# Attention and mixture-of-experts attention on one core: a planner that counts instruction fetches, and its new order

## The chip, the cores and the metric

One core of a Trainium2 chip runs the whole program. The metric is the device time of one execution in microseconds (us). The times shown are the median of three runs; the profile is of one further execution.

## The reference, cut to what matters

Causal softmax attention over 4 batches of 12 heads (448 positions, 64 wide); its output, heads side by side (768 wide), is the input x of a layer of four experts, each a causal attention head of its own, of which a gate takes two per position.

```python
scores = scale * q @ k.T ; causal mask ; a = softmax(scores) ; x = a @ v      # 48 heads
logits = x @ w_gate                     # the two best of 4 experts, softmax over them: w
for e in range(4):
    q, k, v = x @ wq[e], x @ wk[e], x @ wv[e]
    ye = softmax(causal(scale * q @ k.T)) @ v @ wo[e]
    out += chosen_e * w_e * ye
```

All is float32. The projections split weights and x into a high and a low part and take three products (fp32r); scores and softmax times v are plain fp32, whose matmuls the trace records twice.

## The kernel before, in words

The kernel is written as a list of 1540 steps (`Op`), each with the engines that can take it, a duration for each, the steps it comes after, and the buffers that it uses. Nothing is looped over at run time: `Plan.run` goes through the steps in the hand-kept list `ORDER`, gives each to the engine that would end it first by the planner's own clock (or to the one that `CHOSEN` pins), finds buffers, and emits the instructions there and then. So `ORDER` sets, for every engine, the order of its queue, and which buffer a step reuses. The durations (`T_...` and the numbers in `add(...)`) are never seen by the chip; they steer only which engine and which buffer a step gets.

Heads go in pairs: one "member" is two heads (64 partitions each), numbered 0 to 23 for the first layer (6 a batch); members 24 to 31 are the second layer's (batch, experts two by two). A "couple" of two members shares a softmax for the last 64 rows. By name, with the engine that runs them:

- `s1`, `s2` (TensorE, line 532): the scores of one block of 128 rows, and of two blocks; 20 and 40 instructions (weight loads and matmuls). `sq` (line 562): the last 64 rows of a couple, 16 instructions. These and `pv` use TensorE in quarters of 64 x 64.
- `max` (VectorE, line 444), `exp` (ScalarE, line 450), `eps` and `r` (sum and reciprocal), `rg` (GpSimd, times the gate), `norm` (GpSimd or ScalarE, lines 362 and 360): the softmax.
- The turn of the probabilities: for most couples `tr` on VectorE (line 478) and four quarter moves by DMA; for the couples 0 and 4 of the first layer and for the last one (members 30 and 31) transposes `tr` on TensorE (line 501, up to four blocks each) and a copy `mv` out of PSUM by ScalarE or VectorE.
- `pv` (TensorE, line 653): a couple's probabilities times v, 68 calls of matmul, which are 272 instructions. `xh`, `xl`, `xr`: its result copied out in a high and a low part.
- `pj` (line 714): a third of a projection to q or k, 12 instructions. `pjv` (line 761): half of a projection to v and gate, 18 or 12. `pjo` (line 857): the output projection, 12 (in the last batch in two halves of 6). `hb`, `vb`, `ob`: their copies; `gate`: the choice of experts (lines 814 to 839).
- `ld`, `wl`, `mv`, `st`: DMAs, all issued from SyncE's queue (one at the start from ScalarE's).

A step's number after the colon (pv:14) is its first member; pj, pjv and pjo count by batch. The planner's `run` adds `SWITCH` where TensorE changes between whole-array and quarter steps, doubles TensorE's durations before `COLD`, and adds fixed lags between engines. It knows nothing of how instructions reach the engines. Six warm-up matmuls (line 919, 24 instructions) go ahead of the first step of TensorE.

Of the kernel before, what the change touches and what calls it, by code (L numbers as in the profile page):

```python
# [35 lines left out]
class Op:  # L36
    def __init__(self, name, kind, on, emit, after, bufs):
        self.name, self.kind, self.on, self.emit = name, kind, dict(on), emit
        self.after = [a for a in after if a is not None]
        self.bufs = list(bufs)  # L40
        self.size, self.depth = 0.0, 0.0
        if "DMA" in on:
            self.on["DMA"], self.size, self.depth = on["DMA"]
        self.end, self.engine, self.tiling = 0.0, None, 0
        for b in self.bufs:
            b.users += 1
# [11 lines left out]
class Plan:  # L58
# [7 lines left out]
    FROM_PE, FROM_REST, FROM_DMA, SWITCH = 0.22, 0.2, 0.1, 0.11  # L66
    LANDING = 2.0
    SHARED = ("lo", "w", "norm")

    def __init__(self, homes):  # L70
        self.ops = []
        self.homes = homes

    def add(self, name, kind, on, emit, after=(), bufs=(), tiling=0):
        op = Op(name, kind, on, emit, after, bufs)
        op.tiling = tiling
        self.ops.append(op)
        return op

    def seen(self, ops, e):  # L80
        lag = {"PE": self.FROM_PE, "DMA": self.FROM_DMA}
        return max((a.end + (lag.get(a.engine, self.FROM_REST) if a.engine != e or e == "DMA" else 0.0) for a in ops), default=0.0)

# [15 lines left out]
    def run(self, order, chosen, make, tiles):  # L99
        free = dict(self.BEGIN)  # L100
        slots = defaultdict(list)
        copied, last = self.BEGIN["DMA"], None
        for n in order:
            op = self.ops[n]
# [17 lines left out]
            if e == "PE":  # L122
                last = op
            if port:
                free["port"] = end
# [14 lines left out]
def tile_attention_then_moe_attention(  # L140
# [85 lines left out]
    class Make:  # L226
# [12 lines left out]
    QUARTERS = 1  # L239
    LAST = (B - 1,)  # L240
    GROUPS = ((1,), (0, 2))
    ORDER = (
# [726 lines left out]
```

## Time and profile before

| what | us |
|---|---|
| median of 3 runs | 265.44 (264.3 to 267.62) |
| the profiled execution's own time | 263.77 |
| its span, first to last instruction | 262.0 |
| TensorE busy | 249.5 |
| VectorE busy | 203.0 |
| ScalarE busy | 175.4 |
| GpSimd busy | 137.0 |

In the rows PE is TensorE's matmuls, PEld its weight loads, DVE VectorE, ACT ScalarE, POOL GpSimd, SP SyncE. The span was profiled on the one core; its granted TensorE clock is 0.998 of full speed over the span. "issue" is idle time in which an engine waited for nothing that the profile shows. Ends of matmuls are modelled, so short waits between them can lie inside TensorE's busy time.

### The profile page before, as it was taken

The numbers are of one execution on the slowest core, as the hardware profiler recorded it, in microseconds if no ns is written. First come the engines' busy times: TensorE is split into PE (matmuls) and PEld (weight loads), VectorE is DVE, ScalarE is ACT, GpSimd is POOL, SyncE is SP. The second block draws the span as 40 slices with busy tenths as digits, with TensorE's granted clock in tenths as the row PEclk, the third lists the DMA queues.
The fourth block names the chain that finished last, engine by engine and source line by source line (L and its number), as shares of the span: only waits on it lengthen the run. The fifth ranks groups of instructions, "written<-read, shape, count | busy, mean of one in ns | idle before, by whom it ended". The sixth has DMA issues, their size and how long they took to land.

```text
span 262.0 us, 10480 instructions
## 1 busy us (share of the span) xinstructions
PE 249.5 (95%) x4065; PEld 215.8 (82%) x4065; DVE 203.0 (77%) x725; ACT 175.4 (67%) x600; POOL 137.0 (52%) x303
## 2 busy tenths in 40 slices
PE   7999997699999999999998999999999999999992
PEld 5678786579988879998987888989789898989892
DVE  5999999388879998899896998779796654574221
ACT  3999999849465879488584798546365533973321
POOL 6599988479961177975901854860801700043000
PEclk9999999999999999999999999999999999999999
DMA  6997889579878888788858548978868157013317
GB/s 200 397 399 228 206 229 345 191 211 239 220 165 218 232 269 195 220 201 254 256 163 221 139 110 228 271 219 229 200 168 195 34 116 172 0 53 121 115 70 280
DMA packets 34177, 52.27 MB, mean 199 GB/s; under 512 B 3664, under 2 KB 30160, under 8 KB 34128
## 3 DMA queue, kind: packets, MB, share of 16 engines
q1 hardware_dynamic: 33984, 51.47, 68.7%
q8 instruction: 32, 0.52, 0.8%
q10 hardware_dynamic: 144, 0.13, 0.2%
q14 instruction: 17, 0.14, 0.2%
HBM read 19.67 MB, written 5.51 MB: 96 GB/s over the span
## 4 chain that ended last, share of the span: by engine, by line
PE 92%; ACT 3%; issue 3%; DVE 0%; DVEq 0%
PE ps L714 23%; PE ps L653 20%; PE ps L532 15%; PE ps L761 13%; PE ps L857 11%; PE ps L562 5%; PE ps L501 4%; ACT five L450 2%; PE ps L919 1%; ACT tee L450 0%; ACT five L354 0%; DVE raw L356 0%; ACT raw L354 0%; ACT stat L460 0%; DVE five L444 0%
## 5 line engine op out<-in xcount | busy, mean ns | idle before, releaser
L450 ACT ACTIVATE five<-five,stat 128x256 f32<-128x256 f32 (+2 forms) x192 | 95.3, 499 | 33.0 <-DVE stat L444 30.2
L362 POOL TENSOR_SCALAR five<-five,stat 128x128 f32<-128x128 f32 (+2 forms) x171 | 79.7, 486 | 33.0 <-DVE stat L465 16.6
L444 DVE CUSTOM_DVE_ANT_0 five<-ps,mask 128x256 f32<-128x256 f32 (+2 forms) x156 | 59.2, 413 | 15.3 <-PE ps L532 14.9
L714 PE MATMUL ps<-two,wqkh 128*128 128x448 f32 x192 | 55.7, 371 | 0.0
L532 PE MATMUL ps<-raw 64*64 64x128 f32 (+5 forms) x768 | 51.0, 362 | 2.2 <-issue 1.5
L478 DVE STREAM_TRANSPOSE five<-five 128x768 f32<-128x768 f32 x52 | 48.7, 958 | 2.7 <-POOL five L362 1.4
L532 PEld LDWEIGHTS ps<-raw 64*64 64x64 f32 x768 | 32.6, 134 | 12.6 <-issue 6.8
L653 PE MATMUL ps<-five,v 64*64 64x64 f32 (+2 forms) x960 | 38.2, 277 | 1.7 <-issue 1.6
L714 PEld LDWEIGHTS ps<-two,wqkh 128*128 128x128 f32 x192 | 34.4, 188 | 4.2 <-DVE two L356 0.7
L450 ACT ACTIVATION_READ_ACCUMULATOR five<-five,stat 128x1 f32 x192 | 36.4, 190 | 0.0
L653 PEld LDWEIGHTS ps<-five,v 64*64 64x64 f32 x960 | 31.8, 134 | 4.9 <-issue 2.4
L714 PE MATMUL ps<-two,wqkl 128*128 128x448 f32 x96 | 35.1, 366 | 0.0
L761 PE MATMUL ps<-wvh,two 128*128 128x260 f32 x168 | 33.1, 286 | 0.0
L761 PEld LDWEIGHTS ps<-wvh,two 128*128 128x128 f32 x168 | 27.4, 188 | 2.1 <-issue 1.6
L354 ACT ACTIVATE raw<-ps 128x448 f32<-128x448 f32 (+1 forms) x31 | 15.2, 505 | 19.5 <-PE ps L714 11.2
L857 PE MATMUL ps<-two,woh 128*128 128x448 f32 x96 | 27.8, 371 | 0.0
L761 PE MATMUL ps<-wvl,two 128*128 128x260 f32 x96 | 26.4, 283 | 0.0
L653 PE MATMUL ps<-tee,v 64*64 64x64 f32 x672 | 25.6, 218 | 0.4 <-issue 0.4
L653 PEld LDWEIGHTS ps<-tee,v 64*64 64x64 f32 x672 | 23.3, 134 | 1.0 <-issue 0.5
L532 PE MATMUL ps<-warm 64*64 64x64 bf16 x192 | 21.7, 190 | 2.2 <-issue 2.2
L366 DVE TENSOR_TENSOR two<-ps,two 128x448 fp32r<-128x448 f32 x32 | 19.1, 616 | 5.3 <-ACT two L354 5.1
L450 ACT ACTIVATE tee<-tee,stat 128x448 f32<-128x448 f32 x32 | 21.0, 659 | 1.0 <-DVE stat L444 1.0
(93 smaller groups left out, 443.0 us busy)
## 6 DMA issues: line engine op xcount, KB each, us to landing
five<-five SPq DMA_DIRECT2D x104, 192.0 KB, 3.7
raw<-in_qk_dram SPq DMA_DIRECT2D x23, 448.0 KB, 6.0
tee<-tee SPq DMA_DIRECT2D x52, 112.0 KB, 3.5
v<-in_v_dram SPq DMA_DIRECT2D x24, 224.0 KB, 4.3
out_dram<-raw SPq DMA_DIRECT2D x9, 448.0 KB, 2.8
raw<-in_wqk_dram SPq DMA_DIRECT2D x4, 384.0 KB, 6.3
out_dram<-raw SPq DMA_DIRECT2D x6, 224.0 KB, 2.8
raw<-in_wvg_dram SPq DMA_DIRECT2D x2, 390.0 KB, 6.0
```

The costliest lines, as they stand in the source:

```text
L354: nc.scalar.activation(out, in_, AF.Copy)
L362: (nc.gpsimd if e == "POOL" else nc.vector).tensor_scalar(t, t, r, 1.0, op0=ALU.mult, op1=ALU.mult)
L366: eng.tensor_tensor(out=out, in0=a, in1=b, op=ALU.subtract)
L444: lambda e: nc.vector.tensor_tensor_reduce(out=w(), in0=scored(), in1=masked(), scale=-0.125, scalar=3.0e38, op0=ALU.add, op1=ALU.min, acc ...
L450: lambda e: nc.scalar.activation(w(), w(), AF.Exp, bias=stat.at[:, 0, u:u + 1], scale=-1.0, accum_out=stat.at[:, 1, u:u + 1],), [mx], [sto ...
L478: nc.vector.transpose(grouped(mid.at)[:, ks], squares(store.at)[:, ks])
L532: nc.tensor.matmul(out(c, h, lo, hi), lhs, rhs, start=(c, h) not in first, stop=True, skip_group_check=True)
L562: nc.tensor.matmul(tails[h ^ m.n].at[sides[m.n], :S], t.at[sides[h], REM:REM + R], t.at[sides[h], KEY], start=True, stop=True,)
L653: nc.tensor.matmul(o, ms[n].vals(h, k), t, start=(step == 0), stop=(step == len(runs[0]) - 1), skip_group_check=True)
L714: nc.tensor.matmul(ps.at[:, :S], w[:, 2 * sel + p, k], halves(xbuf[b, k].at, t), start=(k == 0 and n == 0), stop=(k == NP - 1 and n == 2),)
L761: nc.tensor.matmul(ps.at[:, :VC], xbuf[b, k].at[:, at + c * P:at + c * P + P], w[:, k], start=(k == 0 and n == 0), stop=(k == NP - 1 and n ...
L857: nc.tensor.matmul(ps.at[:, :S], w[:, p, m * P:m * P + P], halves(ubuf[b, p].at, t), start=(p == 0 and n == 0), stop=(p == 1 and n == 2),)
```

## The change

The planner gets a model of how TensorE's instructions arrive: blocks of 256, asked for 64 ahead of a block's end, 6.0 us each and one behind another; a step that reads over a boundary before its block is there is given a later end. Each TensorE step carries its number of instructions (`words`). Some durations are corrected. `ORDER` and `CHOSEN` are replaced by lists searched with this planner. The steps themselves, their instructions and their dependences are the same.

```diff
-    FROM_PE, FROM_REST, FROM_DMA, SWITCH = 0.22, 0.2, 0.1, 0.11
+    FROM_PE, FROM_REST, FROM_DMA, SWITCH = 0.22, 0.2, 0.1, 0.14
+    BLOCK, AHEAD, FETCH, FIRST = 256, 64, 6.0, 30
...
+        self.read, self.asked, self.needed, self.coming = self.FIRST, self.BLOCK - self.AHEAD, 2 * self.BLOCK, []
...
+    def fetch(self, start, d, words):
+        late, end = 0.0, self.read + words
+        while min(self.asked, self.needed) <= end:
+            at = min(self.asked, self.needed)
+            now = start + d * (at - self.read) / words + late
+            if at == self.asked:
+                self.coming.append(max([now] + self.coming) + self.FETCH)
+                self.asked += self.BLOCK
+            else:
+                late += max(0.0, self.coming.pop(0) - now)
+                self.needed += self.BLOCK
+        self.read = end
+        return d + late
...
             if e == "PE":
                 last = op
+                end = start + self.fetch(start, end - start, op.words)
...
-    T_EXP = (0.39, 0.50, 0.60, 0.71)
-    T_NORM = (0.35, 0.46, 0.57, 0.67)
-    T_NORMA = (0.29, 0.40, 0.51, 0.62)
+    T_EXP = (0.39, 0.495, 0.60, 0.655)
+    T_NORM = (0.35, 0.46, 0.56, 0.62)
+    T_NORMA = (0.30, 0.40, 0.51, 0.57)
-    T_TURNT = 1.02
+    T_TURNT = 1.035
...
-            add(("vb", NC * b + c), "vx", {"POOL": 0.5, "ACT": 0.45}, lambda e: cross(e, 0), made[:NF], [vb, vx]),
+            add(("vb", NC * b + c), "vx", {"POOL": 0.6, "ACT": 0.45}, lambda e: cross(e, 0), made[:NF], [vb, vx]),
...
-        return made, add(("gate", b), "gate", {"DVE": 1.3}, rest, [x], [gt, big])
+        return made, add(("gate", b), "gate", {"DVE": 1.5}, rest, [x], [gt, big])
```

Words given: s1 20, s2 40, sq 16, pv 4 x 68, pj 12, pjv 6 for each of its terms, pjo 12 or 6, transposes 2 for each block. Steps pinned to an engine: ScalarE 81 before and 92 after, VectorE 26 and 26, GpSimd 51 and 50.

The order of TensorE's 231 steps, read out of the two lists (x2: twice in a row). Before:

```
s1:0x3 s1:1 sq:0 s2:1 sq:2 s2:2 s1:3 s1:2 tr:0 s1:4 s1:5 sq:4 s2:4 tr:0 s2:3 tr:0 tr:1 tr:0x2 s2:5 tr:1x2 s2:7 s1:7
pv:0 tr:4 sq:8 s1:8 sq:6 s2:8 tr:4 pj:1 pj:0 s2:6 s1:6 tr:4x3 tr:5x3 s2:9 s1:9 pv:2 sq:10 pv:4 s2:10 s1:10 pj:0 pj:1
pj:0 s2:11 sq:12 s1:11 pj:1 pjv:0x2 pjv:2 pj:2 pjv:2 pjv:1x2 pj:2 s1:24 s2:24 pv:6 s2:12 s1:12 pjv:3 pj:3x2 pj:2 pj:3
s1:13 s2:13 pv:8 sq:24 s1:15 pjv:3 pj:5 s1:25 s2:25 s2:15 pj:5 pj:4x2 sq:14 pv:10 s2:14 pjv:5 pjv:6 pjv:5 pj:5 pjv:4x2
pjv:6 pj:4 s1:14 s1:16 sq:16 pv:12 s2:17 s2:16 s1:17 pjv:7x2 pj:6x2 pj:7 pj:6 sq:18 s1:19 pv:24 s1:18 s2:19 s2:18
pj:7x2 pjo:3 pjo:5 pjo:4 pjo:2 sq:26 s1:26 pv:14 s1:27 s2:27 s2:26 pjo:0 pj:9 pjv:8 pj:9 s1:20 s2:20 sq:22 pv:16 sq:20
pj:8x2 s1:21 s2:21 pj:9 pjv:8 pjo:1 pjv:10 pj:8 pjv:10 s2:23 s1:23 pv:18 s1:22 s2:22 pj:10 pj:11x3 pj:10 pjv:11 pjv:9
pj:10 pjv:11 pv:26 s1:28 s2:28 sq:28 pjv:9 pj:14 pjo:6 pjo:8 s2:29 pv:20 s1:29 pj:13 pj:15 pjv:13 pj:15 pj:12 pjv:14
pj:13 pv:22 pj:12 pj:14 pj:13 pj:15 pj:12 pj:14 pjv:14 s1:30 s2:30 s1:31 sq:30 s2:31 pjv:13 pjv:15x2 pjv:12 pjo:11
pjv:12 pjo:7 pv:28 pjo:9 pjo:10 pjo:16 pjo:17 tr:30x3 pjo:15 tr:31x2 tr:30 tr:31 tr:30 pjo:14 pv:30 pjo:12 pjo:13
pjo:21x2 pjo:23 pjo:22 pjo:20x2 pjo:23 pjo:19 pjo:22 pjo:18x2 pjo:19
```

After:

```
s1:0x3 s1:1 sq:0 s1:2 s2:1 s1:3 s2:2 s1:4 sq:2 tr:0x3 s2:4 sq:4 s2:3 s2:5 tr:0 tr:1x2 tr:0 tr:1 s2:7 s1:5 s1:7 pv:0
tr:4x2 sq:8 sq:6 s2:6 s1:6 pj:1 s2:8 s1:8 pj:0 tr:4x3 s2:9 s1:9 pv:2 sq:10 tr:5x3 pj:2 s2:10 pv:4 s1:11 pj:0 pj:2 pj:1
pj:2 pj:1 pj:0 s1:10 s1:12 s2:11 s2:12 s2:24 sq:12 pv:6 pj:3 pjv:3x2 pj:3 pjv:1x2 pj:3 pjv:2 pjv:0 sq:24 pv:8 s2:13
s1:13 pjv:0 pjv:2 s1:25 s2:25 s2:15 pj:5x2 s1:24 sq:14 s1:15 pv:10 s1:14 s2:14 pj:4x2 pjv:4 pj:5 pjv:4 pjv:6x2 pj:4
pjv:5 sq:16 s2:17 s2:16 pv:12 pj:7x2 pjv:7 pj:7 s1:16 s1:17 pjv:5 pj:6 pjv:7 sq:18 pv:24 s1:19 s2:26 s2:19 pj:6x2
pjo:2 s2:18 sq:26 s1:18 pv:14 s2:20 s1:26 pjo:3 pj:9 pjo:5 pjo:1 pj:9 pjo:0 pj:10x2 s1:27 s1:20 s2:27 sq:20 pv:16
s2:21 sq:22 pjo:4 pjv:9 pjv:8 pj:9 pjv:9 pjv:8 pj:10 s2:22 s1:21 s2:23 s1:22 pj:8x3 pj:11x3 pjv:10 s1:23 pv:26 pjv:10
pjv:11x2 s2:28 pv:18 s1:28 s2:29 sq:28 pjo:10 pj:15 pj:13 pjo:11 s1:29 pv:20 pj:12 pj:14x2 pjv:14 pjv:13 pj:13 pv:22
pj:15 pj:12 pj:14 pj:13 pjv:15x2 pjv:14 pj:12 pj:15 pjv:13 sq:30 s1:31 s2:31 pjv:12x2 s1:30 s2:30 pv:28 pjo:6 pjo:8
pjo:9 pjo:7 pjo:16 tr:30 pjo:17 pjo:12 tr:30 tr:31x3 tr:30x3 pjo:15 pv:30 pjo:14 pjo:13 pjo:18 pjo:23 pjo:21 pjo:19x2
pjo:21 pjo:18 pjo:23 pjo:22x2 pjo:20x2
```

## Rows read from the trace of the kernel before

**Rows 1.** The page, part 1: busy us (share of the span) xinstructions.
```profile
PE 249.5 (95%) x4065; PEld 215.8 (82%) x4065; DVE 203.0 (77%) x725; ACT 175.4 (67%) x600; POOL 137.0 (52%) x303
```

**Rows 2.** The waits of TensorE's matmuls: us in total, times, longest us.
```profile
PE ps L532 <- issue: 3.7, 3, 2.2
PE ps L653 <- issue: 2.2, 3, 1.6
PE ps L919 <- DVE warm L917: 1.1, 1, 1.1
PE ps L532 <- DMA raw<-in_qk_dram: 0.6, 1, 0.6
```

**Rows 3.** Windows, ramp, rest: us, busy (xcount) of PE PEld DVE ACT POOL.
```profile
4.08:38.65 34.57, 33.88 (x551) 25.57 (x554) 32.62 (x149) 32.68 (x116) 30.20 (x63) 1.00 0.89 291
38.65:257.40 218.75, 212.71 (x3511) 187.57 (x3503) 167.68 (x569) 141.11 (x484) 104.47 (x229) 1.00 0.67 185
```

**Rows 4.** The chain that ended last: start us, us, what.
```profile
43.33 1.58 issue
...
48.37 2.19 issue
...
94.17 0.10 issue
...
125.65 0.10 issue
...
140.69 0.91 issue
...
170.71 0.39 issue
...
187.20 0.56 issue
...
247.05 0.20 issue
```

**Rows 5.** Windows from wait to wait (columns as in rows 3).
```profile
0.00:44.00 44.00, 41.50 (x722) 32.24 (x723) 39.73 (x175) 39.28 (x139) 36.45 (x80) 1.00 0.87 286
44.00:50.00 6.00, 3.46 (x128) 2.86 (x128) 3.06 (x8) 5.97 (x24) 4.79 (x7) 1.00 0.85 291
50.00:141.20 91.20, 89.94 (x1518) 79.09 (x1517) 80.45 (x279) 63.72 (x223) 54.83 (x116) 1.00 0.79 214
...
187.50:247.15 59.65, 59.28 (x887) 52.22 (x888) 37.29 (x128) 32.08 (x100) 14.80 (x42) 1.00 0.44 115
```

**Rows 6.** The page, part 3: the queue of TensorE's instruction transfers, packets, MB, share.
```profile
q8 instruction: 32, 0.52, 0.8%
```

**Rows 7.** The chain that ended last: pieces that give a step's duration.
```profile
34.46 1.97 PE ps L501 x16
...
63.28 3.23 PE ps L761 x27
...
74.42 4.90 PE ps L714 x24
79.33 1.37 PE ps L532 x21
...
150.17 0.79 PE ps L562 x8
150.95 3.12 PE ps L653 x116
...
247.58 9.82 PE ps L857 x48
```

**Rows 8.** Windows of some 320 instructions (columns as in rows 3).
```profile
38.65:44.00 5.35, 4.68 (x168) 4.04 (x161) 5.05 (x20) 5.32 (x24) 3.96 (x6) 1.00 0.99 362
149.75:154.24 4.49, 4.49 (x165) 3.95 (x160) 4.43 (x19) 4.40 (x20) 1.47 (x7) 1.00 0.37 82
239.70:247.15 7.45, 7.35 (x161) 6.36 (x160) 3.04 (x5) 2.25 (x5) 0.00 (x0) 1.00 0.51 187
```

**Rows 9.** Window from s1:30's end to pv:30 (columns as in rows 3).
```profile
219.10:243.70 24.60, 24.60 (x321) 22.12 (x313) 16.48 (x65) 15.48 (x50) 5.90 (x16) 1.00 0.24 75
```

More of the change, by code (lines that the diff above doesn't have):

```diff
@@ L36, with __init__ @@
 class Op:
-    def __init__(self, name, kind, on, emit, after, bufs):
+    def __init__(self, name, kind, on, emit, after, bufs, words):
         self.name, self.kind, self.on, self.emit = name, kind, dict(on), emit
@@ L40, in __init__ @@
         self.bufs = list(bufs)
-        self.size, self.depth = 0.0, 0.0
+        self.size, self.depth, self.words = 0.0, 0.0, words
         if "DMA" in on:
@@ L72, in __init__, with add @@
         self.homes = homes
-    def add(self, name, kind, on, emit, after=(), bufs=(), tiling=0):
-        op = Op(name, kind, on, emit, after, bufs)
+        self.read, self.asked, self.needed, self.coming = self.FIRST, self.BLOCK - self.AHEAD, 2 * self.BLOCK, []
+    def add(self, name, kind, on, emit, after=(), bufs=(), tiling=0, words=0):
+        op = Op(name, kind, on, emit, after, bufs, words)
         op.tiling = tiling
@@ L239, in tile_attention_then_moe_attention @@
     QUARTERS = 1
+    WORDS = 68
     LAST = (B - 1,)
@@ L320, in tile_attention_then_moe_attention @@
         "ACT": (
[5 rows of a table removed]
[5 rows of a table added]
         ),
         "DVE": (
-            100, 186, 219, 247, 263, 752, 833, 992, 1001, 1012, 1121, 1140, 1248, 1255, 1258, 1269, 1272, 1296, 1375,
-            1387, 1458, 1460, 1489, 1522, 1533, 1538,
+            183, 217, 749, 1001, 1121, 1123, 1133, 1140, 1148, 1245, 1250, 1253, 1258, 1272, 1276, 1375, 1387, 1408,
+            1462, 1487, 1502, 1512, 1517, 1518, 1523, 1527,
         ),
         "POOL": (
[3 rows of a table removed]
[3 rows of a table added]
         ),
@@ L397, in weight @@
         l = add(("wl", i), "w", {"DMA": (0.45, 1.3, 3.0)}, lambda e: nc.sync.dma_start(t(), src), (), [w])
-        h = add(("wh", i), "w", {"ACT": 0.78, "POOL": 0.87}, lambda e: copy(e, hi, t()), [l], [w])
+        h = add(("wh", i), "w", {"ACT": 0.78, "POOL": 0.81}, lambda e: copy(e, hi, t()), [l], [w])
         split[i] = add(("ws", i), "w", {"POOL": 1.84}, lambda e: sub(e, lo, t(), f32(hi)), [h], [w])
@@ L501, in tr @@
                     nc.tensor.transpose(bank.at[:, at * P:at * P + P], store.at[:, k * P:k * P + P], ident)
-            t = add(("tr", me), "t", {"PE": 0.11 * len(segs)}, tr, [x for k in segs for x in owner(k)], [bank, store])
+            t = add(("tr", me), "t", {"PE": 0.11 * len(segs)}, tr, [x for k in segs for x in owner(k)], [bank, store], 0, 2 * len(segs))
             moved.append(add(("mv", me), "pt", MOVE,
@@ L543, in scores @@
             s = add(("s%d" % len(group), m.me), "s", {"PE": T_SCORE[group]}, mm,
-                    m.ready[:1] if m.first and max(group) < 2 else m.ready, banks + [raw], QUARTERS)
+                    m.ready[:1] if m.first and max(group) < 2 else m.ready, banks + [raw], QUARTERS, 20 * len(group))
             for i in group:
@@ L564, in last @@
                     )
-        s = add(("sq", one), "sq", {"PE": T_QUAD}, last, ms[0].ready + ms[1].ready, tails + [m.raw for m in ms], QUARTERS)
+        s = add(("sq", one), "sq", {"PE": T_QUAD}, last, ms[0].ready + ms[1].ready, tails + [m.raw for m in ms], QUARTERS, 16)
         ends, moved = [], []
@@ L656, in attention @@
         held = [x for m in ms for x in m.v_ready[1]]
-        a = add(("pv", one), "pv", {"PE": T_PV}, pv, moved + ready, accs + ends + [tpt] + held + [m.dest for m in ms], QUARTERS)
+        a = add(("pv", one), "pv", {"PE": T_PV}, pv, moved + ready, accs + ends + [tpt] + held + [m.dest for m in ms], QUARTERS, 4 * WORDS)
         out = []
@@ L719, in second_layer @@
                     after = [xdone[b, k] for k in ks] + [prev, split[2 * sel + p]]
-                    prev = add(("pj", 4 * b + 2 * p + sel), "pj", {"PE": 1.24}, mm, after, [ps] + [xbuf[b, k] for k in ks])
+                    prev = add(("pj", 4 * b + 2 * p + sel), "pj", {"PE": 1.235}, mm, after, [ps] + [xbuf[b, k] for k in ks], 0, 12)
                 o = opsb[p]
@@ L766, in values @@
                 after = [xdone[b, k] if c < NF else xrest[b, k] for k in ks] + [prev, split[4 + part]]
-                prev = add(("pjv", NC * b + c), "pjv", {"PE": 0.36 * len(terms)}, mm, after, [ps] + [xbuf[b, k] for k in ks])
+                prev = add(("pjv", NC * b + c), "pjv", {"PE": 0.36 * len(terms)}, mm, after, [ps] + [xbuf[b, k] for k in ks], 0, 6 * len(terms))
             if c < NF:
@@ L793, in values @@
         made += [
-            add(("vb", NC * b + c), "vx", {"POOL": 0.5, "ACT": 0.45}, lambda e: cross(e, 0), made[:NF], [vb, vx]),
-            add(("vb", NC * b + c), "vx", {"POOL": 0.6, "ACT": 0.55}, lambda e: cross(e, 1), made[:], [vb, vx]),
+            add(("vb", NC * b + c), "vx", {"POOL": 0.6, "ACT": 0.45}, lambda e: cross(e, 0), made[:NF], [vb, vx]),
+            add(("vb", NC * b + c), "vx", {"POOL": 0.7, "ACT": 0.55}, lambda e: cross(e, 1), made[:], [vb, vx]),
         ]
@@ L862, in output @@
                 after = [udone[b, p] for p in ks] + [split[6 + p] for p in ks] + [prev]
-                prev = add(("pjo", 6 * b + m), "pjo", {"PE": 0.615 * len(ks)}, mm, after, [ps] + [ubuf[b, p] for p in ks])
+                prev = add(("pjo", 6 * b + m), "pjo", {"PE": 0.615 * len(ks)}, mm, after, [ps] + [ubuf[b, p] for p in ks], 0, 6 * len(ks))
             if b == B - 1:
```

166 rows, old and new, of tables (CHOSEN, ORDER) are left out of this document.

## The prediction

> **What bounds the kernel now.** I read four views. First the engines' busy time: TensorE is at work 249.5 of 262.0 us, VectorE, ScalarE and GpSimd 203.0, 175.4 and 137.0 [rows 1], so TensorE's own queue sets the end. Then the waits of TensorE: beside its first start (1.1 us) and one load (0.6 us) all its idle time is called "issue", 3.7 + 2.2 us in six waits [rows 2]. "Issue" means that no semaphore held it. Then the two stretches before and behind the third softmax-times-v step: 34.57 us for the ramp, in which VectorE and ScalarE are as full as TensorE (32.6 and 32.7 us), and 218.75 us in which TensorE alone is full [rows 3]. Last the chain of waits, which shows where the six waits lie: 1.58, 2.19, 0.91, 0.39, 0.56 and 0.20 us, with two of 0.10 beside them, 6.0 us in all, each in or right behind a step pv, the one with the most instructions for its time [rows 4].
>
> What are these waits? The windows from one wait to the next count 128 + 128 matmuls and weight loads between the first two, then 1518 + 1517, and 887 + 888 between the last two that I show [rows 5]. That is 256, 3035 and 1775: always a little less than a multiple of 256 (3072, 1792). The missing 37 and 17 would be semaphore instructions, which these counts leave out. And the queue of instruction transfers moved 0.52 MB in 32 packets, one per 254 of the 8130 counted instructions [rows 1, 6]. So TensorE waits for blocks of 256 instructions, and a wait can only fall where such a block begins.
>
> [...]
>
> **The change, part by part.** It runs the same 1540 steps and issues the same instructions: nothing is removed or added on the chip. Moved are the order of all queues and, for some steps, the engine. What can be gained or lost is idle time.
>
> *Sum of the work.* From the chain: four parts of pj take 4.90 us (1.23 each), three of pjv 3.23 (1.08), two of pjo and twelve halves 9.82 (1.23 each whole), a pv 3.12 to 3.3 (I take 3.15), four transposes 1.97, an s1 and an s2 1.37 with the step into them (0.39 + 0.83 + 0.1), sq 0.79 [rows 7]. Over all 231 steps of TensorE this is 232.0 us in either order. Changes between whole-array and quarter steps are 49 before and 47 after, at 0.1 us: 0.2 us won.
>
> *Fetches.* The planner has a block asked for 320 instructions ahead of its need. Going back about that many from a wait gives what a block takes from asking to use: 44.91 - 38.65 = 6.3 us, 247.25 - 239.70 = 7.5, and once, with no wait seen, under 4.5 [rows 4, 8]; while one block is under way the next comes 5.6 us behind it (44.91 to 50.55, rows 4). I lay the steps out one after another with the durations above, put block boundaries where rows 5 have them, and let each block come the same time after its ask, 4.7 us at least behind the one before. As a control, the old order with 5.2 us gives shortfalls of 1.0 (in pv:4), 1.6 (s2:10), 0.75 (s1:27), 0.3 (sq:20), 1.1 (pv:18) and 0.9 (s2:28), 5.6 us in all. Measured are 6.0 at five of these six places, so 5.2 is the value nearest to the rows.
>
> The new order breaks the worst passage: between pv:2 and pv:4 stood one sq (0.8 us), now sq, three transposes, a pj and an s2 (4.3 us), and behind pv:4 come an s1 and six pj instead of an s2 and an s1. The 1.58 + 2.19 us there go. But other passages get denser: with 5.2 us the boundaries that fall into pv:6, s2:13, s2:20 (behind pv:14), s2:21 (behind pv:16) and s1:28 (behind pv:18) have 5.1, 4.9, 4.0, 4.5 and 4.3 us from ask to need. Shortfalls: 0.1 + 0.3 + 1.2 + 0.7 + 0.9 = 3.2 us. At other waits, old against new: 4.5 us 2.3 and 0.6; 5.5 us 7.1 and 4.7; 6.1 us 10.1 and 8.6. The difference stays at 1.5 to 2.5 us. I take 2.0, which leaves some 4 us of fetch waits.
>
> Why not all 6? The count in the planner isn't where the chip's is. It starts at 30, leaves out the 24 warm-up instructions and every semaphore instruction. Up to the first wait the trace counts 722 + 723 [rows 5], so the planner stands at 1445 - 24 + 30 = 1451 where the chip begins a block; its own boundary is at 1536, 85 later. With those 37 and 17 and the rest left out, the gap is 159 at the last wait. So the search kept dense passages clear of boundaries that aren't there: with boundaries where the planner has them, the same layout gives the new order no shortfall at 5.2 us and 0.2 at 6.1, the old one 4.4.
>
> *Corrected durations* (exp, norm, vx, gate) change no instruction, only what the search believes; they act through the order. *Engines:* ScalarE has 92 pinned steps for 81, GpSimd 50 for 51. In the ramp ScalarE's 32.7 of 34.57 us [rows 3] bound the gain at 1.9 us, and the same 26 TensorE steps stand ahead of the first pv; I count nothing. Behind it the steps and switches come to 207.1 us of 218.75: 6.0 are fetches, 5.7 lie inside what the trace counts as busy, so a gain ends there; as much may be lost. I count nothing for these either, since the order leaves nearly as much TensorE work as before between a pair's last scores and its pv (in the layout 23.0 us at the least before, 21.2 after, of the pairs turned on VectorE), which covers softmax, transposes and the moves in SyncE's queue. All loads, quarter moves and stores still go through that queue, in a new order; the cover for a late one is the same 21 us.
>
> *Sum.* 263.77 us is the profiled execution's own time, 262.0 its span with 1.8 around it. Less 2.0 and 0.2 is 261.6. The median of the runs shown is 265.44, 1.7 above that execution; against it the forecast is 265.4 - 2.2 = 263.2 us.
>
> **Rivals.**
> 1. *The count is near enough.* Waits of blocks come to 0.2 us, as with the planner's boundaries, instead of 4: 265.4 - 5.8 - 0.2 = 259.4. For it: the worst passage is gone, and short waits elsewhere on TensorE move asks and needs apart. Against: the 85 to 159 instructions of offset, a third to over half of a block.
> 2. *The last pair comes late* (slower). Place: the transposes and pv:30. Before, 24.6 us lie between the pair's first scores (s1:30) and pv:30, with VectorE busy 16.5 and ScalarE 15.5 of them [rows 9]. In the new order TensorE has work for 21.0 from s1:31 to pv:30: s2 0.8, two pjv 2.2, s1 and s2 1.2, pv:28 3.15, eight pjo 9.9, eight transposes 3.4 and switches 0.4. If the chain maximum, exp, sum, scale, transpose, copy needs its old 24.6 us, pv:30 waits 3.6 us and everything behind it too. It decides from where the chain passes 21.0. With the fetches as they were (no gain), 265.4 + 3.6 = 269; with the forecast's gain 266.8. For it: ScalarE's queue now has the copy behind pjo:9 ahead of the pair's last two exps. Against: the gate values, which held the scales before, are ready sooner, as its pjv:12 moved ahead of s1:30; 16.5 us of VectorE's work fit into 21.
> 3. *The waits aren't fetches,* or come at each block's own whim: then order matters to them little, and the time stays at 265.2 (the switches alone). For it: blocks took from under 4.5 to 7.5 us. Against: the spacing by 256 and the control's places. [...]
>
> **How the numbers follow.** Forecast 0.5, rival 1 0.2, rival 2 0.15, rival 3 0.1, the rest something I don't see. A measurement of this kernel can tell about 2% from no change, here below 260.1 or above 270.7. The forecast's own spread (blocks at 4.5 to 6.1 us, 1.9 us either way in ramp and middle) is 260.5 to 265.5. The range takes in rival 1 and rival 2 with the gain: 259.2 to 267.2. Faster by over 2%: rival 1 mostly (half to two thirds of 0.2) and a corner of the forecast, 0.16; slower by over 2%: a corner of rival 2, 0.04; within 2% 0.80.
>
> **What would show it.** Right: in the chain of the changed kernel no "issue" between pv:2 and the pj behind pv:4; "issue" pieces of 0.3 to 1.5 us right behind pv:14, pv:16, pv:18 and pv:8, 3 to 5 us in all; counts between them again just under multiples of 256. The ramp to pv:2 and the 4.6 us behind the last matmul as before. Wrong: "issue" under 1 us in sum (rival 1); a wait of TensorE on ScalarE, GpSimd or VectorE ahead of the transposes of 30 or of pv:30 (rival 2); "issue" away from pv steps (rival 3); or a ramp that moves by over 2 us, which I cost at nothing.

## The result, and the profile after

The changed kernel took 261.14 us, the median of 20 runs (257.85 to 263.74), against 264.57 for the kernel before (20 runs, 261.4 to 267.62): a ratio of 0.9862, 95% interval 0.9821 to 0.9904. That is 1.4% or some 3.6 us less. The interval leaves out 1, but the change is below the 2% from which a change of this kernel is called faster; the forecast had 2.2 us less. The medians are of all runs, while the ratios, here and below, leave out on either side the runs over 1.5% above the fastest of their kernel, so that the two can differ.

The profiled execution took 263.08 us (span 261.2), near the upper end of its 20, so its trace shows little of the gain. A second profiled execution of the same kernel, beside the experiments below, took 260.18 us (span 258.3), near the median; both are read here. The engines' busy time of the changed kernel, first execution (page, part 1, as [rows 1]):

```profile
PE 248.1 (95%) x4065; PEld 215.4 (82%) x4065; DVE 203.7 (78%) x725; ACT 177.4 (68%) x606; POOL 133.7 (51%) x297
```

Nothing is removed or added: TensorE has the same 4065 matmuls. Some copies went from GpSimd to ScalarE (600 to 606, 303 to 297 instructions). All lines of code stand 20 further down. The waits of TensorE's matmuls, same execution (us in total, times, longest; as [rows 2]):

```profile
PE ps L552 <- issue: 3.2, 2, 1.7
PE ps L673 <- issue: 2.2, 2, 1.6
PE ps L552 <- DMA raw<-in_qk_dram: 1.9, 2, 1.4
...
PE ps L552 <- DVE stat L464: 0.4, 1, 0.4
```

"Issue" has 5.4 us against 5.9 before: four waits instead of six. The chain that ended last says where they lie (start us, us, what; as [rows 4]):

```profile
8.98 1.51 PE ps L552 x18
...
45.83 2.93 PE ps L673 x116
48.76 0.61 issue
...
92.16 1.64 issue
...
124.51 1.55 issue
...
138.00 1.77 issue
```

They are in pv:4 (behind its first 116 matmuls), in pv:10, in s1:19 right behind pv:24 and in s2:20 right behind pv:14. The windows from wait to wait (columns as in rows 3) give the counts, as [rows 5] did:

```profile
49.00:93.00 44.00, 42.80 (x760) 38.16 (x760) 39.45 (x137) 34.78 (x129) 30.09 (x61) 1.00 0.85 229
93.00:125.00 32.00, 30.71 (x504) 26.87 (x505) 25.89 (x84) 21.06 (x71) 19.77 (x44) 1.00 0.79 208
125.00:139.00 14.00, 12.07 (x252) 10.22 (x252) 11.84 (x45) 8.67 (x32) 5.61 (x12) 1.00 0.72 191
```

1520, 1009 and 504 instructions, a little under 1536, 1024 and 512, that is 6, 4 and 2 blocks of 256.

Two more readings of the traces settle that these are waits for instructions. First, counted from 0 over all of TensorE's records, its 106 semaphore and drain instructions too (8236 in all), the instructions that wait are numbers 1473, 1729, 4289, 4801, 5825, 6337 and 8129 before, and 1729, 3265, 4289 and 4801 here: each is 193 plus a whole multiple of 256. Second, the trace holds the 32 transfers of queue q8 [rows 6] one by one, 16384 bytes each, and every such wait ends shortly behind the end of one: before, a transfer from 42.47 to 43.38 us stands ahead of the wait that ends at 44.91, one from 48.13 to 49.01 ahead of 50.55. In the fourteen traces of this case all 52 waits of TensorE over 0.08 us that no semaphore explains stand at 193 plus a multiple of 256, and end 1.2 to 1.6 us behind a transfer.

Now the chain of the second execution:

```profile
8.54 1.51 PE ps L552 x18
...
48.45 1.32 issue
...
65.19 0.47 issue
...
93.46 0.41 issue
...
136.29 0.65 issue
...
153.56 0.30 issue
```

Three of the places are the same (pv:4, pv:10, s2:20), two are others that the forecast had named (pv:6, and s2:21 behind pv:16), and the wait behind pv:24 is missing. The sum is 3.15 us instead of 5.57. That is 2.42 of the 2.90 us between the two executions; 0.44 more came in the ramp (8.98 against 8.54 in the first row). So between these two executions the difference is mostly the fetch waits; two don't show that it is so for the spread of all 20. Why one block can wait in one execution and not in another is seen in the stretch of some 320 instructions ahead of it. That a block is asked for 320 ahead is the planner's figure: no row shows the asking, and in the traces of the kernel before and of the changed kernel no transfer begins more than 285 instructions ahead of the block that it brings. The stretches that end in pv:10, behind pv:24 and behind pv:14, first execution:

```profile
86.00:93.80 7.80, 6.16 (x160) 5.28 (x158) 6.16 (x33) 6.67 (x26) 3.91 (x10) 1.00 0.79 240
118.25:126.06 7.81, 6.26 (x159) 5.10 (x158) 5.78 (x17) 6.25 (x23) 2.67 (x7) 1.00 0.82 201
133.38:139.78 6.40, 4.75 (x165) 4.00 (x158) 5.25 (x20) 5.91 (x22) 0.72 (x2) 1.00 0.84 253
```

and the second:

```profile
87.29:93.87 6.58, 6.17 (x159) 5.28 (x157) 6.00 (x32) 6.46 (x25) 3.14 (x8) 1.00 0.95 267
118.30:124.34 6.04, 6.04 (x159) 5.00 (x161) 5.55 (x15) 5.50 (x21) 1.03 (x3) 1.00 0.82 206
131.67:136.94 5.27, 4.75 (x165) 3.99 (x158) 5.27 (x20) 4.90 (x19) 0.00 (x0) 1.00 0.91 277
```

TensorE's work in each is the same (4.75 and 4.75 in the last), but the stretch took 7.8 and 6.6, 7.8 and at most 6.0, 6.4 and 5.3 us. The DMA engines' share (the last but one number) doesn't explain it here: it is no lower in the second. Nor do the transfers themselves: they took 0.90, 0.96 and 0.95 us in the first and 0.91, 0.96 and 1.36 in the second. What differs is the time before they begin, 5.35, 5.39 and 4.03 us from the start of the stretch against 4.20, 3.71 and 2.74; what a transfer waits for in it stays open.

### The profile page after: what moved, and what is told of

It reads as the page before. It is cut to its first block, busy times and chain, and to the rows that moved or that the text cites. A ratio compares the mean times of both kernels' runs of the same rounds, so it can differ in the third digit from the quotient of the medians.

```text
span 261.2 us, 10494 instructions
## 1 busy us (share of the span) xinstructions
PE 248.1 (95%) x4065; PEld 215.4 (82%) x4065; DVE 203.7 (78%) x725; ACT 177.4 (68%) x606; POOL 133.7 (51%) x297
## 4 chain that ended last, share of the span: by engine, by line
PE 81%; DVE 9%; DMA 3%; issue 3%; SPq 1%; ACT 0%
PE ps L734 23%; PE ps L673 17%; PE ps L552 12%; PE ps L877 12%; PE ps L781 11%; DVE five L464 5%; PE ps L582 4%; DMA raw<-in_qk_dram 3%; PE ps L521 2%; DVE five L498 2%; DVE tee L464 1%; DMA tee<-tee 1%; DVE two L386 1%; DVE tee L498 0%; DVE stat L464 0%
## 5 line engine op out<-in xcount | busy, mean ns | idle before, releaser
L464 DVE CUSTOM_DVE_ANT_0 five<-ps,mask 128x128 f32<-128x128 f32 (+2 forms) x156 | 58.9, 414 | 12.3 <-PE ps L552 10.7
L552 PE MATMUL ps<-raw 64*64 64x64 f32 (+5 forms) x768 | 48.5, 362 | 5.5 <-issue 3.2
L552 PEld LDWEIGHTS ps<-raw 64*64 64x64 f32 x768 | 31.1, 134 | 15.4 <-issue 6.4
L374 ACT ACTIVATE raw<-ps 128x448 f32<-128x448 f32 (+1 forms) x29 | 13.8, 494 | 20.9 <-PE ps L734 12.3
L374 ACT ACTIVATE two<-ps 128x448 fp32r<-128x448 f32 x24 | 12.4, 536 | 18.4 <-PE ps L673 18.3
```

The source lines that it names most:

```text
L374: nc.scalar.activation(out, in_, AF.Copy)
L464: lambda e: nc.vector.tensor_tensor_reduce(out=w(), in0=scored(), in1=masked(), scale=-0.125, scalar=3.0e38, op0=ALU.add, op1=ALU.min, acc ...
L552: nc.tensor.matmul(out(c, h, lo, hi), lhs, rhs, start=(c, h) not in first, stop=True, skip_group_check=True)
```

## The experiments

The theory (A): TensorE waits where a block of 256 of its instructions begins, if the passage before is denser than the block's arrival; order and count decide. Rivals: the waits are something else or random (as rival 3), or other parts of the change (ramp, choice of engines, durations) made the difference. The changed kernel was run again, and the kernel before alongside in every group.

**The changed kernel again.**

> The changed kernel as it is, again, beside the next three on the same chip: for a second profile. Fetch waits 3 to 5.5 us at the places of its first profile (pv:4, pv:10, behind pv:24, behind pv:14; now and then s2:13), each of another size; time about 261.

260.21 us (6 runs), 0.984 [0.9799, 0.988]: the gain is there again. Its profile is the second execution above, with waits at three of the four places expected.

**Planner's durations and count alone, with the old lists.** (First entries of two lists.)

```diff
-    ORDER = (26, 32, 0, 33, 34, 35, 37, 40, 36, 27,
+    ORDER = (26, 0, 32, 33, 34, 37, 35, 36, 27, 40,
...
-        "ACT": (18, 24, 58, 60, 84, 86, 88, 98, 102, 173,
+        "ACT": (12, 58, 60, 75, 84, 86, 88, 98, 102, 105,
```

> The changed planner (corrected durations, fetch count) with the old order and choice: only a few unpinned steps change engine (two copies of a pv's result go from VectorE to ScalarE, some scalings between GpSimd and ScalarE). Expected the time of the kernel before, 264 to 265.5, and its fetch waits at its places: durations and count do nothing by themselves. If the corrected durations carried the gain: 262 or less.

264.29 us, 1.0015 [0.9975, 1.0055]: nothing. All that the planner learned acts through the two lists. Its profiled execution took 263.80 us, and the chain has:

```profile
43.61 1.53 issue
...
48.60 1.91 issue
...
140.62 1.25 issue
```

With 0.60 at 125.10, 0.25 at 170.97, 0.41 at 187.25 and 0.16 at 247.09 that is 6.1 us, at the places of [rows 4]: the old order has its waits at the same seven instructions in a second execution.

**128 more instructions in the ramp.** 64 matmuls of zeros and 64 weight loads more in the first member, which add nothing to any value; the count of all that follows moves by half a block.

```diff
-                        put(early, h, z, z, wide - HD, wide)
+                        for _ in range(33 if m.first and i == 2 else 1):
+                            put(early, h, z, z, wide - HD, wide)
```

> The changed kernel with 128 more instructions on TensorE: the zero matmuls of the first member's third score step are repeated 32 times more for each half, so that every later block boundary falls 128 instructions earlier in the order, near to where the planner has it. Theory A (waits depend on where the boundaries fall; the planner has them 85 to 159 instructions off): fetch waits fall from 5.5 us to about 0.3 to 0.7 us, the time from 261.1 to about 257 (the repeats cost 0 to 1.5 us in the ramp, where TensorE waits for loads anyway). Theory B (a block comes late at its own whim, the boundary's place doesn't matter): fetch waits stay at 4 to 6 us, the time at 261 to 262.5.

262.32 us, 0.9972 [0.9922, 1.0021]. The chain around the only long "issue":

```profile
41.39 3.05 issue
...
45.88 1.46 PE ps L521 x12
47.34 1.23 PE ps L735 x6
```

(Another 0.89 at 64.88 is a wait for VectorE by the waits of TensorE.) None of the four places of the changed kernel waits any more; one wait appears 7 us earlier, in pv:2. Another order of steps isn't needed to move the waits: 128 instructions do it. That is theory A, and against rival 3. The size was missed: 3.05 us of waits are left, as many as in the changed kernel's second execution, and the time is not lower. By the planner's count of 320 instructions this block took 9.9 us from asking to use, with the DMA engines at 0.90:

```profile
34.55:44.45 9.90, 6.85 (x159) 6.15 (x157) 5.96 (x35) 9.06 (x35) 7.57 (x14) 1.00 0.90 318
```

**64 and 224 more instructions.** The same edit with 17 and 57 in place of 33.

> The same with 64 more instructions (16 repeats for each half). Theory A: fetch waits 0.6 to 2.5 us, the time about 258 to 259. Theory B: 4 to 6 us and 261 to 262.

262.13 us, 0.9946 [0.9896, 0.9997], one long "issue", in sq:10 behind pv:2:

```profile
41.82 2.44 issue
...
45.22 2.54 PE ps L521 x12
47.77 1.75 PE ps L735 x6
```

The place follows the count once more. The three transposes and the pj behind it took 4.29 us here and 2.69 in the kernel with 128 more (rows above); the last section comes back to that.

> The same with 224 more instructions (56 repeats for each half). Theory A: the boundaries fall into the new order's dense passages; fetch waits grow from 5.5 us to 8.5 to 10 us, the time to 265 to 268. Theory B: fetch waits stay at 4 to 6 us, the time is 1 to 3 us above the changed kernel, for the repeats alone.

267.88 us (4 runs), 1.02 [1.0104, 1.0297], the slowest of the three, in the range of theory A. TensorE's waits in its profiled execution:

```profile
PE ps L552 <- issue: 4.4, 4, 2.3
...
PE ps L674 <- issue: 0.5, 1, 0.5
```

4.9 us in five waits: not the 8.5 to 10 of theory A, but between the changed kernel's 3.15 and 5.57, and in the range of theory B. TensorE's busy time is 253.1 us, 4.0 more than in the second execution of the changed kernel (249.1), and this execution, 265.81 us, was the fastest of its four. So most of the loss seen here is not fetch waits, and this run doesn't show that they grow.

**128 more instructions in the kernel before.** The same edit in the old order.

> The kernel before with 128 more instructions in the same place. Theory A: fetch waits fall from 6.0 to 3.3 to 4.5 us, less than in the changed kernel, since the old order was not searched for any place of the boundaries; time 262 to 264. Theory B: fetch waits stay near 6 us, time 264.5 to 266.

262.64 us, 0.9973 [0.9919, 1.0026]. "Issue" in the chain:

```profile
43.51 2.07 issue
...
49.35 0.77 issue
...
101.95 1.25 issue
```

With 0.69 at 116.62 and 0.60 at 197.71 that is 5.4 us: the later places are all new ones, while the dense pair pv:2 and pv:4 keeps two waits, now at two other instructions. This execution, 264.16 us, is the slowest of the ten. By the ratio the shift does nothing in the old order; by the medians of all runs it is 2.5 us below the kernel before of the same group (265.12). And it is level with the new order with the same 128 instructions (262.32), which matters for the account below.

**Loads moved back.** The loads of 13, 14 and 20 go further back in SyncE's queue, to thin out the transfers at 34 to 41 us. The edit moves three of the 1540 entries of `ORDER`; here SyncE's queue is read out around them. In the trace three loads that were issued at 36.9 to 42.4 us go to some 48, 60 and 74.

```diff
-    v:6   ld:13  mv:6
+    ld:12 ld:13  mv:7
...
-    v:4   ld:14  wl:3
+    v:11  ld:14  ld:15
...
-    wl:3  ld:20  v:7
+    v:17  ld:20  mv:10
```

> The changed kernel with three loads of q and k (members 13, 14 and 20, 448 KB each, not needed before 76, 91 and 143 us) moved back in SyncE's queue, out of 34 to 45 us, where the DMA engines are full and a block took 6.6 to 10 us from ask to use against 4 to 5 elsewhere. Theory C (a block is late because it queues behind data): the fetch wait in pv:4 (0.6 us) goes, the ramp loses up to 1 us less, the waits behind 60 us (1.6, 1.6, 1.7) stay; time 260 to 261. Theory B (own whim): no change at any place beyond its scatter, 261 to 262.

261.37 us, 0.9876 [0.9776, 0.9976], as the changed kernel. In its chain pv:4 has 0.15 us of "issue", but there are others, 2.19 us in s2:13, 0.71 in pv:10 and 2.07 in s2:20 (profiled execution 264.29 us, the slowest of the four).

> The same with 96 more instructions (24 repeats for each half in the first member's third score step). Theory A and C together: with 64 and with 128 more instructions one wait of 2.4 and 3.1 us was left, at 42 to 44 us where the DMA engines were full; with the loads moved it falls under 1 us, no other fetch wait is above 0.5, and the time is 258 to 259.5 (waits of 5.5 us fall by 4 to 5, the repeats cost about 1). Theory B: 4 to 6 us of waits, 261 to 263. If only A holds and not C: one wait of 2 to 3 us is left at 42 to 44 us, 261 to 262.

The same with 96 more instructions: 261.58 us, 0.9891 [0.9836, 0.9946]. Its long wait is again in pv:2, 2.63 us at 41.16. So fewer loads there did not cure the wait in pv:2. The burst was thinned only in part (the DMA engines were at 0.67 over the 320 instructions ahead of that block), so that the transfers delay the block is neither shown nor refuted.

**Old ramp, new rest.** The first 255 entries of the old list (to s1:6, some 34 us), with their engines, then the new order. (First line of the list.)

```diff
-        26, 32, 0, 33, 34, 35, 37, 40, 36, 27, 38, 41, 39, 29, 42, 43, 44, 45,
+        26, 0, 32, 33, 34, 37, 35, 36, 27, 40, 38, 39, 42, 41, 29, 61, 45, 46,
```

> The old order up to its step s1:6 (about 34 us), the new one from there. In the profiles the ramp to 35 us lost 4.7 us before and 5.8 after (over the sum of the steps' durations). If the ramp is a part in which the new order loses, this kernel is 1 us faster than the changed one, 260; if the difference was the loads' scatter (the first loads landed 0.7 to 1.4 us later in that execution), the same, 261. Fetch waits as after: 3 to 5.5 us.

261.06 us, 0.9882 [0.9793, 0.9971]: the same as the changed kernel. The gain isn't in the ramp. In its chain two fetch waits stand out, 1.06 us in pv:10 and 2.28 in s2:20, as in the changed kernel.

**New order with the old choice of engines.** (First line of ScalarE's list.)

```diff
-            18, 24, 58, 60, 84, 86, 88, 98, 102, 173, 176, 185, 186, 188, 219, 254,
+            12, 58, 60, 75, 84, 86, 88, 98, 102, 105, 107, 127, 221, 236, 334, 397,
```

> The new order with the old list of engines for the pinned steps. If the gain of the changed kernel is in the order of TensorE alone, 261 to 262 with fetch waits at the same places; if the new choice of engines carries part of it, a wait of TensorE on ScalarE, GpSimd or VectorE shows and the time is 263 or more.

268.82 us, 1.0184 [1.0093, 1.0276], 7.7 us slower than the changed kernel. The waits of TensorE:

```profile
PE ps L673 <- issue: 2.2, 2, 1.8
PE ps L552 <- DVE gate L376: 1.3, 1, 1.3
PE ps L552 <- issue: 1.2, 2, 0.6
PE ps L673 <- DMA five<-five: 1.1, 2, 0.9
...
PE ps L521 <- POOL tee L382: 0.8, 1, 0.8
```

The "issue" waits stay about as they were. The line of `DVE gate` is in truth a fetch wait for the most part: it stands at instruction 4289, in s1:19, where the changed kernel waits 1.55 us; the gate's copy ended at 129.09 us, TensorE went on at 129.93, 1.32 us behind a transfer of instructions. New are waits for quarter moves, GpSimd and ScalarE, and TensorE's busy time is 4.2 us longer (253.3 against 249.1), in which short waits can lie. Order and choice belong together.

**Lists searched with the boundaries where the trace has them.** A search of our own over order and choice, with the changed planner's model, but with the count started at 90 instead of 30, words taken 1.3% higher for the semaphore instructions, and arrivals as in the traces. Two of the lists were run (first line of each).

```diff
-        26, 32, 0, 33, 34, 35, 37, 40, 36, 27, 38, 41, 39, 29, 42, 43, 44, 45,
+        26, 0, 1, 27, 32, 35, 36, 33, 34, 37, 40, 38, 39, 42, 45, 41, 46, 29,
```

> The same planner and steps, but order and choice searched with the blocks where the trace has them: the count starts at 90 instead of 30 at the first step, 1.3% is added for semaphore instructions, a block comes 5.2 or 6.5 us after its ask and 4.7 us behind the one before. By this count the list has no fetch wait and ends at 251.5 us of the planner's clock (the changed kernel 254.2 with 2.9 us of waits at 5.2 us); by the count of the change it would have 12.9 us of waits and end at 264.4, against 251.3 for the changed kernel. Theory A: fetch waits under 1.5 us, time 257 to 259.5. If the planner's own count were right: over 8 us of waits and 268 or more. Theory B: waits of 4 to 6 us, 261 to 263.

264.45 us (12 runs, 260.82 to 267.41), 0.9987 [0.9943, 1.0031]. Its waits in the profiled execution:

```profile
PE ps L465 <- DMA raw<-in_qk_dram: 1.4, 2, 0.9
...
PE ps L465 <- DVE stat L377: 1.1, 2, 0.5
PE ps L586 <- issue: 0.6, 2, 0.5
```

The fetch waits are nearly gone, and this execution, 260.82 us, is the fastest of the twelve. What the others lose, up to 6.6 us, isn't in this trace and stays open.

```diff
-        26, 32, 0, 33, 34, 35, 37, 40, 36, 27, 38, 41, 39, 29, 42, 43, 44, 45,
+        26, 32, 27, 0, 33, 34, 35, 110, 37, 40, 41, 38, 39, 29, 36, 42, 45, 46,
```

> A second list of the same search from another start: no wait at 5.2 us and 0.5 at 6.5 us, end 252.3 to 252.8 of the planner's clock (12.4 us of waits by the count of the change). Theory A: 258 to 260.5, fetch waits under 2 us. Planner's own count: 268. Theory B: 261 to 263.

261.16 us (4 runs), 0.9864 [0.9811, 0.9917], the same as the changed kernel. Its waits:

```profile
PE ps L465 <- DVE stat L377: 1.4, 2, 0.8
PE ps L465 <- DMA raw<-in_qk_dram: 1.4, 1, 1.4
PE ps L434 <- DVE stat L377: 1.1, 1, 1.1
...
PE ps L465 <- ACT five L287: 0.6, 1, 0.6
PE ps L586 <- issue: 0.3, 1, 0.3
```

With the boundaries where the chip has them a search does clear the fetch waits, in the one execution profiled of each list (0.6 and 0.3 us). But 4.5 us of waits for data stand in the ramp and behind it, twice those of the changed kernel's first execution (2.3). No list beat the changed kernel.

## Why the prediction was right or wrong

- *TensorE's fetches bound what the order can gain: right.* Every wait over 0.08 us without a semaphore stands at the same place of a block (193 plus a multiple of 256) and ends 1.2 to 1.6 us behind a transfer of instructions, the old order repeats its waits in a second execution, and added instructions move them. Most blocks cost nothing: of the 32 places of a block's beginning in the kernel before 25 show no wait, the other seven have 5.9 us.
- *The planner's boundaries are not the chip's: shown.* The chip's stand at 193 plus multiples of 256, four or five waits remain where the planner saw clear passages, and the two lists searched with the trace's boundaries have 0.6 and 0.3 us of them in their profiles. It was not shown that the offset alone costs time, as neither list was faster.
- *The term that was mis-sized: "I take 2.0, which leaves some 4 us of fetch waits".* The two profiled executions nearest to their kernels' medians, old lists with corrected durations (263.80) and the changed kernel again (260.18), have 6.1 and 3.15: 3.0 us less, of 3.62 between the times. By them the mechanism was right and the term 1.0 too small. It hangs on the pair: the first executions, 263.77 and 263.08, have 6.0 and 5.57, 0.5 less, and the new order's two have 4.4 on average, near the 4 forecast. Of the remaining 0.6 us, 0.5 lie behind the last matmul: 4.6 us (257.38 to 262.0) in the old order, 4.1 (254.16 to 258.3) in the new. The prediction had this "as before"; what shortens it wasn't tested. The 0.2 of fewer switches no row shows separately.
- *Where the gain lies, and luck.* In pv:4 and s2:10 behind it the old order lost 3.77 and 3.44 us, the new one loses 0.61 and 1.32 in pv:4. All other fetch waits together are 2.3 and 2.7 us in the old order, 5.0 and 1.8 in the new: no gain is shown there. And here too it matters where the boundaries happen to fall, which the planner had 85 to 159 instructions off: with 128 more instructions the new order waits 3.05 us between pv:2 and the steps behind pv:4, the old one 2.84, and the two take the same time (262.32 and 262.64 us, ten runs each). So part of the gain is luck; how much of it the order would keep at any place of the boundaries stays open.
- The control that chose 5.2 us was read too well. At five of its six places the rows have 5.6 us, not 6.0; the other 0.4 lie at three places that it doesn't have. And no row shows the 4.7 us taken as the least from one block to the next: in the first trace of the changed kernel transfers begin as little as 3.5 us behind one another.
- Behind that stands the one figure of 5.2 us for every block. By the planner's count of 320 instructions, which no run shows, the same block took 7.8 and at most 6.0 us in two executions, others 5.3 to 10. So the predicted places held only in part. s2:20 (1.2 predicted) had 1.77 and 0.65, pv:6 (0.1) 0 and 0.47, s2:21 (0.7) 0 and 0.30; s2:13 and s1:28 had none. Not predicted were pv:10 (1.64 and 0.41) and s1:19 (1.55 and 0). And "the 1.58 + 2.19 us there go" was wrong by the remainder in pv:4, 0.61 and 1.32: the block that begins late in pv:4 still doesn't come in time.
- *Ramp at nothing: right* (old ramp with new rest, 261.06 us). *Durations at nothing by themselves: right* (1.0015).
- *Choice of engines at nothing: right only for the pair.* With the new order the old choice costs 7.7 us. The layout of TensorE's steps in the prediction didn't see this, as the waits lie in other engines' queues.
- *Rival 1* (0.2 us of waits left, 259.4 us): refuted by the waits, 3.15 and 5.57 us, and by the ratio, 0.977 by its time and 0.986 measured. *Rival 2* (the last pair late): did not occur; no wait of TensorE on another engine is among those of the first execution behind the ramp, and its "issue" ends at 140 us. *Rival 3*: right that each block has its own time, wrong that order and count matter little.
- The forecast had 2.2 us less and the measurement 3.6. The unit against which it was made, 265.44, was itself 0.9 above the later median of 264.57.

## What to carry to other kernels

Where TensorE runs many short instructions (8236 here), count them, with the semaphore instructions, between idle pieces that have no releaser. In this case all 52 such waits over 0.08 us stood at 193 plus a multiple of 256 and ended 1.2 to 1.6 us behind a transfer of the instruction queue, and half a block of padding in front (128 instructions) moved them from all four places of the changed kernel. A planner that is to avoid such waits here needs the count of the trace, with warm-up and semaphore instructions: without them it was 85 to 159 off. It also needs a margin for the spread between executions, 7.80 and 6.58 us for the same stretch. One profiled execution can stand at either end of the spread, 257.85 to 263.74 us here, so read two before a term of 1 us is believed.

## What the runs showed of the hardware that was not expected

The time to the beginning of a block varied between two executions of one program by more than a microsecond (7.80 and 6.58 us, 6.40 and 5.27 us for the same instructions). The fetch waits make 2.42 of the 2.90 us between the two profiled executions of the changed kernel, as much as two thirds of the whole gain.

TensorE's granted clock fell in the middle of the kernel after a fetch wait. In the kernel with 64 more instructions, behind the wait of 2.44 us at 41.82 (windows, columns as in rows 3):

```profile
43.00:46.00 3.00, 1.74 (x8) 1.04 (x9) 0.74 (x4) 0.00 (x0) 0.00 (x0) 0.90 0.96 337
46.00:49.00 3.00, 3.00 (x14) 2.86 (x13) 2.17 (x5) 1.88 (x6) 2.91 (x6) 0.53 0.18 57
49.00:52.00 3.00, 3.00 (x87) 2.20 (x89) 1.92 (x7) 2.96 (x10) 0.96 (x3) 1.00 0.81 214
```

The granted clock was 0.90 and then 0.53 of full speed; from 40 to 43 us and from 49 to 52 it was 1.00. TensorE had stood still for 2.44 us before. The transposes and the pj there took 4.29 us, 1.6 us longer than behind the 3.05 us wait of the kernel with 128 more (2.69), where the clock stayed at 1.00:

```profile
44.50:47.50 3.00, 3.00 (x49) 2.28 (x50) 2.39 (x8) 0.81 (x3) 0.40 (x2) 1.00 0.44 135
```

It fell, to 0.50, in two more traces, each with loads moved back: behind the 2.63 us wait in pv:2 (with 96 more instructions) and behind the one of 2.19 us in s2:13 (with none added):

```profile
45.50:48.50 3.00, 3.00 (x13) 2.87 (x13) 2.79 (x8) 1.74 (x5) 2.29 (x6) 0.50 0.41 144
...
82.00:84.50 2.50, 2.50 (x19) 2.12 (x12) 2.33 (x12) 0.00 (x0) 0.00 (x0) 0.50 0.92 244
```

So one fetch wait cost 1.6 us more than its own length, and the longer one of 3.05 us did not. What decides it, these runs don't show.
